# HGRN2 attention and rational MoE: units of one batch, decay products on GpSimd, a new order

## The chip, the cores and the metric

The kernel runs on one NeuronCore of a Trainium2 chip. Its five engines work at the same time, each through its own queue in order: TensorE (PE in the profile, with PEld for the weight loads), VectorE (DVE), ScalarE (ACT), GpSimd (POOL) and SyncE (SP). They wait for one another through semaphores. SP issues most of the loads and all stores; POOL issues the loads that change type, and the transfers that add. The metric is the device time of one execution in microseconds; lower is better.

## The reference

The input is 4 batches, 8 heads, 768 tokens, 48 values a head. First comes a linear attention with a decaying state, then a feed-forward layer (384 to 2048 to 384) whose activation is a quotient of polynomials:

```python
f = 1 / (1 + exp(-f_logit))
for t in range(S):
    state = f[:, :, t, :, None] * state + einsum('bhd,bhe->bhde', k[:, :, t], v[:, :, t])
    y[:, :, t] = einsum('bhd,bhde->bhe', q[:, :, t], state)
x = y.transpose(0, 2, 1, 3).reshape(B * S, H * D)
h = x @ w_in
P = a[0] + a[1]*h + a[2]*h**2 + a[3]*h**3
Q = 1 + abs(b[0])*abs(h) + abs(b[1])*h**2
out = (P / (Q + 1e-6)) @ w_out
```

## The kernel before

The work is cut into 12 units of 256 tokens. A unit `n` takes 128 successive tokens of two batches (j = 0 and 1). One partition holds two successive tokens of one batch, so that 64 partitions belong to each j. Units alternate between the two pairs of batches, and each pair has one state tile, renewed once a unit.

The order of the instructions is written out by hand: the string `ORDER` (lines 19 to 104) lists steps, and the loop at its end (line 560) issues them one by one. Each engine keeps this order in its own queue. `@0` to `@3` names one of four PSUM slots (two banks each). A step `name n ...` belongs to unit n.

The attention steps of a unit:

- `ld` loads f, k, q (SP) and v (POOL, as bf16), one transfer for each j (line 194). Unit 0 loads its heads in two halves.
- `ef` and `ls` (ACT, lines 279 and 284) make log(1 + exp(-f)) in place and into `lsp`; `cs` (PE, line 294) sums it over the tokens with triangular matrices; `A` (ACT, lines 304 and 306) takes exp of the sums, once for q (x = 0) and once for k (x = 1), each into one tile with a single buffer.
- `xa` (DVE, line 311) multiplies q or k by its `A`, 128x768 f32 by f32 into the bf16 tile `qkp`.
- `T` (PE, line 322) transposes them, `Te` (DVE, line 330) copies the result out of PSUM; `sc` (PE, line 343) forms the scores, `mk` (DVE, line 351) masks them; `vm` (POOL, line 358) packs a part of v.
- `ya` and `yb` (PE, lines 364 to 415) form y in PSUM from the state and from the scores, and the state's sum `sv`. `ae` and `st` (ACT and DVE, lines 425 and 429) multiply that by the last decay `alast` and give the next state. `ye` (ACT, line 420) copies y as the input xT of the feed-forward.

The feed-forward steps, over groups of 4 or 8 of the 16 column blocks:

- `h` (PE, line 438) multiplies by w_in; `hy` (ACT, line 452) copies to bf16; the square is formed by `sq` (DVE, line 456) or by `sa` (ACT, line 460); `ab` (DVE, line 464) takes the absolute value z.
- The denominator is the sum of square and z, and its logarithm is taken on ACT. The sum is formed in one of three ways: by `u`, identity matmuls into PSUM (line 472), read by `ln` (ACT, line 480); by `zv` on DVE (line 485); or by `zd`, a transfer that adds in SBUF (POOL, line 489). The last two are read by `lz` (ACT, line 496). `ex` (ACT, line 504) makes exp(-log).
- The numerator is formed on DVE by `p1`, `p2` and `pm` (lines 509, 514, 519), joined by `tv` (DVE, line 527) or by the adding transfer `ta` (POOL, line 523), and multiplied by `ex` in `gm` (DVE, line 532).
- `o` (PE, line 539) multiplies by w_out, `oe` (line 554) copies the result, `so` (SP, line 548) stores it.

Coefficients are scaled so that the denominator needs no multiplication: the scale of ScalarE's `ln` and the bias of its `A` for q are read from the tile `sig`. At the start VectorE clears whole padded tiles (`cz`), and POOL loads w_in in 8 transfers of 32 partitions (line 201) and w_out in 4 (line 205).

Of the kernel before, what the change touches and what calls it, by code (L numbers as in the profile page):

```python
# [19 lines left out]
cz 1; ld 0 v; ab_; ld 0 q 2 4; cz 0; ld 0 f 2 4; cz 2; cb; ld 0 f 0 2; wi 0 4; ld 0 k 2 4; fa  # L20
ld 0 k 0 2; cz 3; fb; ld 0 q 0 2; ef 0 2 4; ls 0 2 4; vm 0 0; ef 0 0 2; ld 1 f; vm 0 1; ls 0 0 2; ca
wi 4 16; cs 0 2 4 @0; cc; cs 0 0 2 @1; A 0 0 2 4; A 0 1 0 2; xa 0 0 2 4; A 0 1 2 4; A 0 0 0 2
xa 0 1 2 4; ld 1 k; xa 0 1 0 2; T 0 2 4 @1; xa 0 0 0 2; ld 1 q; Te 0 2 4; ld 1 v; T 0 0 2 @0
sc 0 1 @1; Te 0 0 2; ef 1; ld 2 f; mk 0 1; sc 0 0 @0; ya 0 @2 @3; ls 1; mk 0 0; yb 0 2 4; ae 0
cs 1 @1; st 0; yb 0 0 2; A 1 1; A 1 0; ye 0; h 0 0 4 @2; hy 0 0 4; h 0 4 8 @1; wo 4 8; wo 12 16
h 0 12 16 @2; hy 0 4 8; xa 1 1; ld 2 k; wo 0 4; h 0 8 12 @3; sq 0 0 8; wo 8 12; hy 0 12 16; ld 2 q
ab 0 0 8; hy 0 8 12; xa 1 0; u 0 0 4 @2; ab 0 8 16; T 1 @3; vm 1 0; ln 0 0 4; p1 0 0 8; ld 2 v
u 0 4 8 @1; Te 1; ef 2; ld 3 f; p2 0 0 8; sc 1 1 @3; vm 1 1; ln 0 4 8; sc 1 0 @2; mk 1 1; ls 2
ya 1 @1 @0; mk 1 0; ex 0 0 8; cs 2 @3; sq 0 8 16; yb 1; A 2 1; pm 0 0 8; u 0 12 16 @2; ye 1
p1 0 8 16; ae 1; A 2 0; h 1 0 4 @1; tv 0 0 8; ln 0 12 16; ld 3 k; h 1 12 16 @3; hy 1 0 4; p2 0 8 16  # L30
gm 0 0 8; h 1 4 8 @2; hy 1 12 16; pm 0 8 16; u 0 8 12 @1; hy 1 4 8; xa 2 1; h 1 8 12 @3; ln 0 8 12
tv 0 8 16; o 0 0 0 4 @2; ex 0 8 16; ab 1 0 8; o 0 1 0 4; sq 1 0 8; o 0 0 4 8; ld 3 q; hy 1 8 12
o 0 1 4 8; xa 2 0; u 1 0 4 @1; gm 0 8 16; T 2 @3; ld 3 v; ln 1 0 4; st 1; o 0 1 8 12; o 0 1 12 16
Te 2; ef 3; ld 4 f; vm 2 0; u 1 4 8 @0; vm 2 1; ls 3; sq 1 8 16; sc 2 0 @3; ln 1 4 8; sc 2 1 @1
ld 4 k; o 0 0 8 12; mk 2 0; o 0 0 12 16; ex 1 0 8; cs 3 @0; mk 2 1; ld 4 q; ab 1 8 16; A 3 1
ya 2 @1 @3; p1 1 0 16; A 3 0; vm 3 0; oe 0 0 2 s; yb 2; ld 4 v; xa 3 1; u 1 12 16 @0; ae 2; ye 2
so 0 0 2; p2 1 0 16; u 1 8 12 @2; ef 4; ld 5 f; vm 3 1; ln 1 12 16; h 2 12 16 @1; pm 1 0 8; ls 4
ld 5 k; st 2; h 2 0 4 @0; hy 2 12 16; tv 1 0 8; ln 1 8 12; cs 4 @3; ld 5 q; xa 3 0; h 2 4 8 @1
hy 2 0 4; gm 1 0 8; sa 2 0 4; h 2 8 12 @2; ld 5 v; pm 1 8 16; hy 2 4 8; o 1 0 0 4 @0; hy 2 8 12
ab 2 0 8; o 1 1 0 4; vm 4 1; tv 1 8 16; A 4 0; o 1 0 4 8; vm 4 0; ld 6 f; sa 2 4 8; T 3 @2  # L40
p1 2 0 16; A 4 1; o 1 1 4 8; ld 6 k; ex 1 8 16; xa 4 0; u 2 4 8 @1; Te 3; u 2 0 4 @3; ld 6 q
ln 2 4 8; gm 1 8 16; sc 3 1 @2; ln 2 0 4; sc 3 0 @1; mk 3 1; o 1 0 8 12; ef 5; o 1 1 8 12; mk 3 0
ex 2 0 8; o 1 1 12 16; ya 3 @2 @3; xa 4 1; ld 7 f; pm 2 0 8; ef 6; yb 3; ae 3; ls 5; T 4 @1; ld 7 k
st 3; vm 5 0; vm 5 1; ye 3; o 1 0 12 16; sq 2 8 16; ld 6 v; h 3 0 4 @2; oe 1 0 2 s; ld 7 q; Te 4
h 3 4 8 @0; so 1 0 2; hy 3 0 4; ab 2 8 16; ld 8 f; pm 2 8 16; ef 7; u 2 8 12 @1; hy 3 4 8; sc 4 0 @2
p2 2 0 16; h 3 8 12 @3; ln 2 8 12; ab 3 0 8; ta 2 8 16; u 2 12 16 @0; mk 4 0; hy 3 8 12; ta 2 0 8
cs 5 @1; ln 2 12 16; sq 3 0 8; sc 4 1 @2; h 3 12 16 @3; A 5 1; mk 4 1; zd 3 0 8; A 5 0; hy 3 12 16
xa 5 1; ya 4 @1 @0; ex 2 8 16; xa 5 0; ld 8 k; yb 4; p1 3 0 16; T 5 @3; ld 8 q; ld 7 v; ye 4
ab 3 8 16; ef 8; h 4 0 4 @1; Te 5; ae 4; ls 6; vm 6 0; h 4 4 8 @2; gm 2 8 16; vm 6 1; hy 4 0 4
ld 9 f; sa 4 0 4; pm 3 0 8; h 4 8 12 @3; hy 4 4 8; st 4; h 4 12 16 @1; hy 4 8 12; gm 2 0 8; sa 4 4 8  # L50
sc 5 1 @0; cs 6 @3; sq 3 8 16; hy 4 12 16; o 2 0 0 4 @2; ab 4 0 8; o 2 1 0 4; A 6 1; p2 3 0 16
zd 4 0 8; o 2 1 4 8; A 6 0; u 3 12 16 @1; lz 3 0 8; xa 6 0; ta 3 0 8; o 2 1 8 12; mk 5 1
o 2 1 12 16; ln 3 12 16; u 3 8 12 @3; xa 6 1; ld 9 q; ex 3 0 8; sc 5 0 @0; pm 3 8 16; o 2 0 4 8
ld 9 k; o 2 0 8 12; ab 4 8 16; ta 3 8 16; o 2 0 12 16; ln 3 8 12; p1 4 0 16; T 6 @1; oe 2 0 2 s
mk 5 0; ex 3 8 16; ya 5 @2 @3; so 2 0 2; pm 4 0 8; yb 5; ls 7; Te 6; ld 8 v; ae 5; cs 7 @0; ye 5
ld 10 f; st 5; sc 6 1 @1; lz 4 0 8; h 5 4 8 @2; mk 6 1; vm 7 0; vm 7 1; sc 6 0 @3; sq 4 8 16
hy 5 4 8; h 5 8 12 @1; A 7 0; gm 3 0 8; h 5 0 4 @2; A 7 1; zv 4 8 16; hy 5 8 12; o 3 0 0 4 @0
hy 5 0 4; o 3 0 4 8; pm 4 8 16; o 3 1 0 4; lz 4 8 16; mk 6 0; o 3 1 4 8; h 5 12 16 @2; p2 4 0 16
ef 9; ya 6 @3 @1; ex 4 0 8; ab 5 0 8; ta 4 0 8; gm 3 8 16; ta 4 8 16; yb 6; hy 5 12 16; sq 5 0 8
o 3 1 8 12; ye 6; o 3 1 12 16; p1 5 0 16; zd 5 0 8; ex 4 8 16; o 3 0 8 12; o 3 0 12 16; ld 9 v  # L60
sq 5 8 16; h 6 8 12 @3; ae 6; ls 8; st 6; h 6 12 16 @2; ef 10; vm 8 1; ld 11 f; pm 5 0 8; vm 8 0
hy 6 8 12; cs 8 @1; xa 7 1; hy 6 12 16; h 6 4 8 @3; ab 5 8 16; ld 10 k; oe 3 0 2 s; xa 7 0
u 5 12 16 @2; A 8 1; so 3 0 2; gm 4 0 8; A 8 0; T 7 @0; ld 10 q; ln 5 12 16; xa 8 0; u 5 8 12 @1
hy 6 4 8; Te 7; o 4 0 0 4 @2; ln 5 8 12; o 4 0 4 8; xa 8 1; sc 7 1 @0; sa 6 4 8; o 4 1 0 4
gm 4 8 16; sc 7 0 @1; lz 5 0 8; o 4 1 4 8; p2 5 0 16; o 4 0 8 12; o 4 0 12 16; mk 7 0; ex 5 8 16
ta 5 0 8; T 8 @3; mk 7 1; o 4 1 8 12; o 4 1 12 16; ex 5 0 8; sq 6 8 16; ya 7 @0 @1; pm 5 8 16
ld 11 k; oe 4 0 2 s; yb 7; ae 7; ls 9; Te 8; h 6 0 4 @2; ta 5 8 16; so 4 0 2; ye 7; vm 9 1; st 7
# [12 lines left out]
ls 11; so 6 0 2; cs 10 @3; vm 11 0; st 9; ye 9; u 8 4 8 @2; vm 11 1; gm 7 0 8; A 10 0; u 8 0 4 @0  # L80
A 10 1; pm 7 8 16; o 7 0 0 4 @1; ln 8 4 8; h 9 4 8 @3; sq 8 8 16; ta 7 8 16; ln 8 0 4; o 7 0 4 8
xa 10 0; sa 9 4 8; h 9 12 16 @0; p2 8 0 16; hy 9 4 8; o 7 1 0 4; ex 8 0 8; xa 10 1; ta 8 0 8
o 7 1 4 8; pm 8 8 16; h 9 0 4 @3; hy 9 12 16; gm 7 8 16; ta 8 8 16; T 10 @2; sa 9 0 4; zv 8 8 16
h 9 8 12 @0; hy 9 0 4; Te 10; lz 8 8 16; o 7 1 8 12; o 7 1 12 16; gm 8 0 8; sc 10 1 @2; sc 10 0 @3
hy 9 8 12; o 7 0 8 12; ab 9 0 8; o 7 0 12 16; mk 10 0; ex 8 8 16; zd 9 0 8; o 8 0 0 4 @0; p1 9 0 16
o 8 1 0 4; oe 7 0 2 s; o 8 1 4 8; ab 9 8 16; cs 11 @3; so 7 0 2; gm 8 8 16; ya 10 @1; A 11 0
o 8 0 4 8; mk 10 1; A 11 1; o 8 1 8 12; lz 9 0 8; o 8 0 8 12; xa 11 0; yb 10; sq 9 8 16; o 8 1 12 16
ye 10; o 8 0 12 16; xa 11 1; u 9 12 16 @2; ex 9 0 8; p2 9 0 16; T 11 @1; oe 8 0 2 s; h 10 4 8 @3
pm 9 0 8; ln 9 12 16; so 8 0 2; Te 11; h 10 12 16 @0; ta 9 0 8; hy 10 4 8; pm 9 8 16; sa 10 4 8
sc 11 1 @1; h 10 0 4 @2; mk 11 1; hy 10 12 16; ta 9 8 16; sc 11 0 @3; sa 10 0 4; ya 11 @0; mk 11 0  # L90
h 10 8 12 @1; hy 10 0 4; yb 11; ab 10 0 8; hy 10 8 12; u 9 8 12 @2; gm 9 0 8; ye 11; u 10 0 4 @1
# [21 lines left out]
def kernel(  # L113
# [22 lines left out]
    UB = 2  # L136
# [48 lines left out]
    def load(n, what, a0=0, a1=HP):  # L185
# [4 lines left out]
        if what not in s:  # L190
            s[what] = ld.tile([P, H, 2, D], dt, name=what + "n")
# [402 lines left out]
```

## Time and profile before

| | us |
|---|---|
| median of 3 runs (lowest, highest) | 247.41 (247.39, 249.63) |
| span of the profiled execution, first to last instruction | 244.1 |
| median less span | 3.3 |
| busy: PE, DVE, ACT, POOL | 214.6, 210.6, 204.8, 62.1 |
| `xa` of whole units on DVE, 22 | 21.0 |
| mean rate of the DMA engines | 155 GB/s |

The profile shows one execution. Of it the page gives the span; the time around the span is known only as the 3.3 us between it and the median of the runs. An engine is busy while one of its instructions runs; idle time of an engine is given with what released it. A row of the groups has the engine, the operation, the tiles and shapes, a count behind an x, then the busy time and the mean of one in ns, then the idle time ahead of it. A row of the waits has who waited for whom, the total, how often, and the longest. Transfers that add are listed under the POOL instruction that issues them.

### The profile page before, as it was taken

What the parts mean: (1) busy time and instruction counts of PE and PEld (TensorE: products, weight loads), DVE (VectorE), ACT (ScalarE), POOL (GpSimd) and SP (SyncE); (2) the same over time, 40 slices, a digit from 0 to 9 for tenths busy, and PEclk for the clock granted to TensorE, in tenths of its full rate; (3) what the DMA queues carried; (4) which work ended last, traced back from release to release, by engine and by line L of the source; (5) the groups of instructions that cost most, each with busy time, mean ns of one, the idle gap of its engine ahead of it and who ended that gap; (6) DMA issues with size and microseconds to landing.
All of it is one profiled execution on the core that took longest, in us unless ns stands there. A gap on an engine that the chain in (4) does not pass through costs nothing.

```text
span 244.1 us, 7193 instructions
## 1 busy us (share of the span) xinstructions
PE 214.6 (88%) x3144; PEld 146.9 (60%) x3144; DVE 210.6 (86%) x233; ACT 204.8 (84%) x213; POOL 62.1 (25%) x98
## 2 busy tenths in 40 slices
PE   0228787999998999997999999999999999999991
PEld 0115564765774868665668577668568658666550
DVE  7427179999999999999979999999999998899740
ACT  2422568989999899999799999999999999999930
POOL 7953201500400344233071032242122102004110
PEclk9999997999999999999999999999999999999997
DMA  6999999980799999999989999678529746606972
GB/s 82 217 199 198 204 196 221 208 131 0 127 208 204 166 239 169 201 200 220 161 161 165 232 179 172 101 153 131 105 74 172 145 97 118 121 3 129 199 145 64
DMA packets 61342, 37.94 MB, mean 155 GB/s; under 512 B 52096, under 2 KB 57600, under 8 KB 61312
## 3 DMA queue, kind: packets, MB, share of 16 engines
q0 software_dynamic: 19424, 18.62, 49.3%
q1 hardware_dynamic: 41888, 18.88, 40.1%
q8 instruction: 24, 0.39, 0.7%
q14 instruction: 6, 0.05, 0.1%
HBM read 25.17 MB, written 4.72 MB: 122 GB/s over the span
## 4 chain that ended last, share of the span: by engine, by line
PE 42%; ACT 18%; DMA 13%; DVE 13%; SPq 7%; issue 5%; DVEq 0%; ACTq 0%
PE op L539 15%; PE hp L438 13%; DMA fn<-in_f_logit_dram 8%; SPq L194 7%; DMA gall<-hy 5%; PE u L472 5%; ACT hy L452 4%; DVE gall L532 3%; ACT qi L504 3%; ACT lq L480 3%; PE y L364 2%; PE tp L322 2%; DVE h L456 2%; DVE gall L509 2%; PE sc L343 2%
## 5 line engine op out<-in xcount | busy, mean ns | idle before, releaser
L438 PE MATMUL hp<-xT,w_in_sb 128*128 128x256 bf16 x576 | 67.9, 273 | 1.7 <-ACT xT L420 1.4
L539 PE MATMUL op<-w_out_sb,gall 128*128 128x384 bf16 x384 | 68.4, 326 | 0.9 <-DVE osb L554 0.7
L438 PEld LDWEIGHTS <-w_in_sb 128*128 128x128 bf16 x576 | 55.4, 98 | 11.5 <-issue 2.1
L452 ACT CAST hy<-hp 128x1024 bf16<-128x1024 f32 x48 | 48.5, 1021 | 5.7 <-PE hp L438 5.4
L539 PEld LDWEIGHTS <-gall 128*128 128x128 bf16 x384 | 36.3, 98 | 25.5 <-DVE gall L532 1.2
L504 ACT ACTIVATE qi<-lq 128x2048 bf16<-128x2048 f32 (+1 forms) x25 | 46.5, 1871 | 0.2
L523 POOL DMA_DIRECT2D gall<-hy x21 | 19.5, 960 | 83.6 <-ACT hy L452 14.8
L480 ACT ACTIVATE lq<-u,sig 128x1024 f32<-128x1024 f32 x32 | 35.4, 1134 | 1.2 <-PE u L472 1.1
L532 DVE TENSOR_TENSOR gall<-gall,qi 128x2048 bf16<-128x2048 bf16 (+1 forms) x25 | 29.5, 1182 | 4.1 <-DMA gall<-hy 4.0
L351 DVE TENSOR_TENSOR scm<-sc,mask 128x1024 bf16<-128x1024 f32 x24 | 28.7, 1217 | 1.6 <-PE sc L343 1.6
L519 DVE TENSOR_TENSOR gall<-gall,h 128x2048 bf16<-128x2048 bf16 (+1 forms) x25 | 29.3, 1181 | 0.0
L194 POOL DMA_DIRECT2D vn<-in_v_dram x24 | 18.8, 801 | 27.0 <-issue 20.3
L456 DVE TENSOR_TENSOR h<-hy 128x2048 bf16<-128x2048 bf16 (+1 forms) x19 | 22.2, 1167 | 2.1 <-ACT hy L452 2.1
L294 PE MATMUL cs<-lsp,Ui 128*128 128x384 bf16 (+1 forms) x39 | 11.6, 359 | 12.5 <-ACT lsp L284 12.5
L358 POOL COPY vmp<-vn 128x128 bf16<-128x128 bf16 x24 | 10.7, 483 | 44.0 <-PE y L364 27.9
L279 ACT ACTIVATE fn<-fn 128x768 f32<-128x768 f32 (+1 forms) x13 | 10.7, 823 | 13.3 <-DMA fn<-in_f_logit_dram 13.3
L472 PE MATMUL u<-h,ident 128*128 128x512 bf16 x64 | 19.5, 387 | 0.0
L472 PEld LDWEIGHTS <-ident 128*128 128x128 bf16 x128 | 12.2, 99 | 11.7 <-issue 0.7
L472 PE MATMUL u<-z,ident 128*128 128x512 bf16 x64 | 19.1, 379 | 0.0
L322 PE MATMUL tp<-ident,qkp 128*128 128x128 bf16 x192 | 13.7, 227 | 6.0 <-DVE qkp L311 4.6
L509 DVE TENSOR_SCALAR gall<-hy,a_sb 128x4096 bf16<-128x4096 bf16 (+2 forms) x15 | 17.0, 1142 | 1.6 <-ACT hy L452 1.6
L311 DVE TENSOR_TENSOR qkp<-qn,A 128x768 bf16<-128x768 f32 (+1 forms) x13 | 11.6, 892 | 7.4 <-DMA qn<-in_q_dram 4.1
(70 smaller groups left out, 283.3 us busy)
## 6 DMA issues: line engine op xcount, KB each, us to landing
gall<-hy POOLq DMA_DIRECT2D x19, 512.0 KB, 6.1
fn<-in_f_logit_dram SPq DMA_DIRECT2D x22, 192.0 KB, 7.2
kn<-in_k_dram SPq DMA_DIRECT2D x22, 192.0 KB, 6.9
qn<-in_q_dram SPq DMA_DIRECT2D x22, 192.0 KB, 6.8
out_dram<-osb SPq DMA_DIRECT2D x22, 192.0 KB, 3.7
z<-h POOLq DMA_DIRECT2D x5, 512.0 KB, 6.2
vn<-in_v_dram POOLq DMA_DIRECT2D x24, 96.0 KB, 8.0
w_out_sb<-in_moe_w_out_dram POOLq DMA_DIRECT2D x4, 384.0 KB, 15.9
```

The lines of the kernel that those rows point to most:

```text
L194: eng.dma_start(out=s[what][R * j:R * j + R, hh].rearrange("p h i d -> p h (i d)"), in_=src[s["u"] * UB + j, hh, t0:t0 + C, :].rearrange(" ...
L351: nc.vector.tensor_mul(t, s["sc", g].rearrange("s r a i t -> s (r a) (i t)"), mb)
L438: nc.tensor.matmul(t[:, m - m0, :].rearrange("f (j t) -> f j t", j=UB), w_in_sb[:, kk, m * P:(m + 1) * P], s["x"][:, :, kk, :], start=(kk ...
L452: nc.scalar.copy(fl(big(s, "hy", "hy", 3), m0, m1), fl(s["hp", m0], 0, m1 - m0))
L456: nc.vector.tensor_mul(fl(big(s, "h2", "h2", 2), m0, m1), fl(s["hy"], m0, m1), fl(s["hy"], m0, m1))
L472: nc.tensor.matmul(t[:, m - m0:m - m0 + 2, :].rearrange("p m t -> p (m t)"), ident, fl(src, m, m + 2), start=(x == 0), stop=(x == 1))
L480: nc.scalar.activation(fl(s["lq", g], m0 - 8 * g, m1 - 8 * g), fl(s["u", m0], 0, m1 - m0), AF.Ln, scale=sig[:, 2:3], bias=1.0 + 1e-6)
L504: nc.scalar.activation(fl(s["qi", g], m0 - 8 * g, m1 - 8 * g), fl(s["lq", g], m0 - 8 * g, m1 - 8 * g), AF.Exp, scale=-1.0)
L509: nc.vector.tensor_scalar(fl(big(s, "g", "gall", 3), m0, m1), fl(s["hy"], m0, m1), a_sb[:, 3:4], a_sb[:, 2:3], op0=ALU.mult, op1=ALU.add)
L519: nc.vector.tensor_mul(fl(s["g"], m0, m1), fl(s["g"], m0, m1), fl(s["h2"], m0, m1))
L532: nc.vector.tensor_mul(fl(s["g"], m0, m1), fl(s["g"], m0, m1), fl(s["qi", g], m0 - 8 * g, m1 - 8 * g))
L539: nc.tensor.matmul(s["op"][:, j, 0:DM], s["g"][:, m, C * j:C * j + C], w_out_sb[:, m, :], start=(m == 0), stop=(m == KF - 1))
```

## The change

A unit is now 256 successive tokens of one batch, so j is the first or the second half of 256 tokens of the same batch. One load takes all 128 partitions. The state goes from j = 0 to j = 1 within the unit, so there are two state tiles for each batch, `st` has half the width and is done twice a unit, and `ya` is taken apart into `yi` (y from the state) and `sv`. From unit 1 on, `xa` runs on POOL. A step may carry a name at its end (`!m3`); an `xa` on POOL names one (`p m3`) and is made to begin behind it. Only unit 0 keeps `xa` on DVE, in four halves.

The scales that came from `sig` tiles are now registers of ScalarE, and the bias of `A` is gone (its factor is in `ye`). The memsets clear only the padding. w_in comes in 3 transfers of 128 partitions for each of two column ranges. The order is new: `sa`, `zv`, `tv` and half-size steps are no longer used; the unit's feed-forward uses `u` 24 times (32 before), `ln` 24 (32), `lz` 12 (8), `zd` 12 (5) and `ta` 24 (21, two of them half).

```diff
--- before
+++ after
-cz 1; ld 0 v; ab_; ld 0 q 2 4; cz 0; ld 0 f 2 4; cz 2; cb; ld 0 f 0 2; wi 0 4; ld 0 k 2 4; fa
-ld 0 k 0 2; cz 3; fb; ld 0 q 0 2; ef 0 2 4; ls 0 2 4; vm 0 0; ef 0 0 2; ld 1 f; vm 0 1; ls 0 0 2; ca
+cz 3; ab_ b a; ld 0 f 0 2; ld 0 v; ld 0 f 2 4; cz 1; cu 1; ld 0 k 2 4; cz 2; ci; ld 0 k 0 2; cu 0
+ld 0 q 2 4; ef 0 0 2; wi 4 16; cm; ld 0 q 0 2; ef 0 2 4; cz 0; fa; ls 0 2 4; ls 0 0 2; cs 0 2 4 @3; ld 1 v
...
+xa 1 1 0 4 p m1; A 1 0; yb 0 2 4; ld 2 k; yi 0 1; sv 0 1; ye 0 s; st 0 1; ef 2; h 0 12 16 @2; wi 0 4; ls 2
+ld 3 f; h 0 8 12 @1; hy 0 12 16; xa 1 0 0 4 p m1; cs 2 @3; hy 0 8 12; ld 2 q; A 2 1; wo 4 8; T 1 @2
+ab 0 8 16 !m3; A 2 0; xa 2 1 0 4 p m3; sv 1 0 @1; Te 1; h 0 4 8 @3; ab_ a s; ae 1; st 1 0; vm 1 0; sc 1 1 @2
...
+o 11 0 0 4 @3; o 11 1 0 4; oe 9 0 2 s; gm 11 8 16; o 11 1 4 8; oe 10 0 2 s; so 9 0 2 s; o 11 0 4 8
+o 11 1 8 12; so 10 0 2 s; o 11 0 12 16; o 11 0 8 12; o 11 1 12 16; oe 11 0 2 s; so 11 0 2 s
...
-            c, u = divmod(n, NU)
-            units[n] = dict(c=c, u=u, qk=qkp[n % 2], ls=lsp[n % 2], vm=vmp[n % 2], st=states[u])
+            c, b = divmod(n, B)
+            units[n] = dict(c=c, b=b, qk=qkp[n % 2], ls=lsp[n % 2], vm=vmp[n % 2], st=states[b])
...
-        for j in range(UB):
-            eng.dma_start(out=s[what][R * j:R * j + R, hh].rearrange("p h i d -> p h (i d)"),
-                          in_=src[s["u"] * UB + j, hh, t0:t0 + C, :].rearrange("h (p i) d -> p h (i d)", i=2))
+        eng.dma_start(out=s[what][:, hh].rearrange("p h i d -> p h (i d)"),
+                      in_=src[s["b"], hh, t0:t0 + NT, :].rearrange("h (p i) d -> p h (i d)", i=2))
...
-        if x == 0:
-            nc.scalar.activation(t, src, AF.Exp, scale=-1.0, bias=sig[:, 3:4])
-        else:
-            nc.scalar.activation(t, src, AF.Exp, scale=1.0)
+        nc.scalar.activation(t, src, AF.Exp, scale=1.0 if x else -1.0)
-    def xa(n, x, a0=0, a1=HP):
+    def xa(n, x, a0=0, a1=HP, eng="v", mark=None):
...
-        nc.vector.tensor_mul(s["qk"][:, x, :, hh, 0:D],
+        i = (nc.gpsimd if eng == "p" else nc.vector).tensor_mul(
+            s["qk"][:, x, :, hh, 0:D],
...
+        if mark is not None:
+            behind(i, mark)
+        return i
...
+    def coef_r():
+        for i in (0, 2):
+            regs[i] = nc.scalar.alloc_register(f"sig{i}")
+            nc.scalar.reg_load(regs[i], sig[0:1, i:i + 1].bitcast(U32))
...
+    def yi(n, j, sl=None):
+        s = unit(n)
+        y_open(s, sl)
+        for kk in range(KD):
+            for a in range(HP):
+                ymm(s, j, a, kk, s["st"][j][:, a, 32 * kk:32 * kk + 32], s["T"][:, 0, :, a, R * j:R * j + R])
...
-    def st(n):
-        s = unit(n)
-        nc.vector.tensor_mul(s["st"], s["sv"], _at(s["ae"], [[1, UB], [UB, HP], [0, 2 * D]]))
+    def st(n, j):
+        s = unit(n)
+        return nc.vector.tensor_mul(s["st"][1 - j], s["sv"][:, j], _at(s["ae"], [[UB, HP], [0, W]], j))
...
-                             scale=sig[:, 2:3], bias=1.0 + 1e-6)
+                             scale=regs[2], bias=1.0 + 1e-6)
...
+    def behind(i, mark):
+        tc.add_manual_dep(i.ins, marks[mark].ins.name,
+                          mybir.DependencyInfo(mybir.DependencyClass.Sync, mybir.DependencyReason.DATA),
+                          reason="begins behind it")
```

## The prediction

> **What bounds the kernel now.** I read the busy shares of the page first, then the table by stage, then the waits and the groups.
>
> ```profile
> PE 214.6 (88%) x3144; PEld 146.9 (60%) x3144; DVE 210.6 (86%) x233; ACT 204.8 (84%) x213; POOL 62.1 (25%) x98
> ```
>
> Three engines lie within 5% of each other, so the shares name no bound. I cut the span at the end of unit 1's copy `ye` (43 us) and at the next-to-last output copy (233.5 us).
>
> ```profile
> 0.00:43.00 43.00, 22.60 (x382) 15.37 (x383) 25.58 (x50) 19.88 (x27) 17.36 (x39) 0.97 1.18 188
> 43.00:233.50 190.50, 186.64 (x2733) 128.65 (x2732) 183.11 (x181) 183.63 (x185) 44.77 (x60) 1.00 0.86 151
> 233.50:244.10 10.60, 5.40 (x32) 2.87 (x30) 1.94 (x3) 1.29 (x3) 0.00 (x0) 0.87 0.43 97
> ```
>
> The columns are length, then busy time of PE, PEld, DVE, ACT and POOL, the granted clock, the DMA share and GB/s. In the middle PE is busy 98%, DVE and ACT 96% each: nothing is gained there unless all three get less to do. In the first 43 us they are busy about half, while the DMA moves 188 GB/s: the start waits for data. The waits say for which.
>
> ```profile
> ACT fn L279 <- DMA fn<-in_f_logit_dram: 13.3, 4, 7.9
> PE cs L294 <- ACT lsp L284: 12.5, 4, 10.0
> DVE qkp L311 <- DMA qn<-in_q_dram: 4.1, 2, 3.7
> DVE qkp L311 <- DMA kn<-in_k_dram: 3.9, 1, 3.9
> ```
>
> So there are two accounts: the start (order of loads) and the middle (work of three engines). The sum is made against the span of 244.1; the median of the runs, 247.41, is 3.3 more, and I carry that 3.3 over.
>
> **The middle, engine by engine.** Rows first (the last number ahead of the bar is the count; behind it busy us and mean ns):
>
> ```profile
> L311 DVE TENSOR_TENSOR qkp<-kn,A 128x768 bf16<-128x768 f32 x11 | 10.5, 958 | 3.9 <-DMA kn<-in_k_dram 3.9
> L311 DVE TENSOR_TENSOR qkp<-qn,A 128x768 bf16<-128x768 f32 x11 | 10.5, 952 | 0.6 <-DMA qn<-in_q_dram 0.4 <-ACT A L304 0.2
> L456 DVE TENSOR_TENSOR h<-hy 128x2048 bf16<-128x2048 bf16 x17 | 20.8, 1223 | 2.1 <-ACT hy L452 2.1
> L460 ACT ACTIVATE h<-hp 128x1024 bf16<-128x1024 f32 x12 | 12.6, 1053 | 0.2 <-PE hp L438 0.2
> L480 ACT ACTIVATE lq<-u,sig 128x1024 f32<-128x1024 f32 x32 | 35.4, 1134 | 1.2 <-PE u L472 1.1
> L496 ACT ACTIVATE lq<-z,sig 128x2048 f32<-128x2048 bf16 x8 | 16.2, 2024 | 0.0
> ```
>
> *PE.* The order forms the denominator by identity matmuls (`u`) 24 times, not 32. The chain shows one `u` as 0.86 us: 8 x 0.86 = 6.9 less. The sums for `alast` are made for 12 units, not 10: 16 matmuls more, 0.28 us for 8 in the chain. PE: -6.3.
>
> *ACT.* The 12 squares `sa` go (-12.6). `ln` falls from 32 to 24 (-9.1), `lz` rises from 8 to 12 (+8.1). The 11 whole `A` of q lose their bias, 921 against 828 ns (-1.0). An output copy comes back from DVE and `alast` has two more (+0.7). The scale of `ln`, now a register, I cost at nothing: both ends, 0 and 24 x 0.11 (the gap from the 1134 to the 1021 of `hy`) = -2.6, lie on an engine with slack. ACT: -14.
>
> *DVE.* 22 products `xa` leave (-21.0), so do 3 `zv` (-3.6), 4 `tv` (-4.9) and one output copy (-0.6). Squares rise from 20.8 + 1.4 to 24 x 1.223 (+7.2). The state product becomes 20 of half width; at 0.56 (a 128x384 copy from PSUM, 558 ns) that is 11.2 against 9.5 (+1.7). Fewer, longer `p1` and `p2` give -1.4; smaller memsets help only the start. DVE: -22.6.
>
> *What the 22 products cost on POOL.* No row shows POOL multiplying two f32 tensors. Ends: 0.95 us (the same work on DVE) and 3.5 us (POOL's copy `vmp`, 128x128 in 0.29 us, scaled by 768/128 and doubled for the second input). I take that copy scaled by size alone, 1.74 us, as the nearest row of that engine. 22 x 1.74 = 38 us on POOL, which is idle for 146 of the middle's 190 us; its 12 fewer loads of v at 0.80 take 9.6 back. So POOL has the time; the question is DVE:
>
> ```profile
> 42.34 0.81 DVE L509 TENSOR_SCALAR gall<-hy,a_sb 128x2048 bf16<-128x2048 bf16 x1
> 42.58 1.85 POOL L358 COPY vmp<-vn 128x128 bf16<-128x128 bf16 x1 [4.24 <-PE y L364]
> 43.06 1.22 DVE L527 TENSOR_TENSOR gall<-gall,hy 128x2048 bf16<-128x2048 bf16 x1
> 44.19 0.81 DVE L514 TENSOR_SCALAR hy<-hy,a_sb 128x2048 bf16<-128x2048 bf16 x1
> ```
>
> A POOL copy of 0.29 us took 1.85 us, and ended only as the two DVE steps over it did. DVE shut POOL out. Beside DVE steps that read PSUM (`mk` at 22.05 us, `st` at 23.87, 80.66 and 162.22) the same copy keeps 0.29 to 0.31 us. The other way round the trace shows little: the DVE steps over slow POOL copies grew by at most 0.2 us (a `p1` of 1.53 against 1.34), but those copies are short. I take it that a product beside a PSUM-reading step costs nothing, and beside any other holds DVE for all its length. The order places the 22 products ahead of: 18 times `mk`, `Te` or `st`, 4 times a step on SBUF. Adding the PSUM steps that follow each without a gap (`mk` and `Te` 1.22, `st` 0.56): five have 1.78, eight 1.22, five 0.56, four none, together 21.5 us of cover. Blocked: 38.3 - 21.5 = 17 us. Ends: 0 (POOL always yields or DVE is idle) and 77 - 21.5 = 56 (3.5 us each). DVE: -22.6 + 17 = -5.6.
>
> The Trainium skill ("SBUF — State Buffer", section "SBUF: two separate sides") says that DVE steps with two SBUF inputs or in a two-port mode and GpSimd steps hold one port pair exclusively, for the whole instruction. The row agrees (0.29 became 1.85). "GPSIMD Engine Reference", section 3, speaks against the change: it calls the engine the wrong choice for elementwise work, at 4497 ns for 2048 f32 pairs. An estimate from that page is 1.69 us for 768, which would make the blocked time 16 us and the sum 1 us less.
>
> *Waits that are added.* A product waits for its `A`, its load and its named step. In the order 13 of the 22 names lie over 30 DVE steps back; in the built program three products carry a wait on DVE. Behind a waiting product on POOL stand DMA additions `ta` and `zd`; `gm` (DVE) and `lz` (ACT) wait for those. `A` has one buffer, so ACT's next `A` waits for POOL as well. I price this at nothing, covered by the lead of the attention (units 2 and 3 are begun before unit 0's output): uncovered, it costs the 1.74 of a product for each, 38 us at most.
>
> *DMA.* Additions rise from 25 full-size equivalents to 36, +5.8 MB. The middle moved 151 GB/s x 190.5 = 28.8 MB; 34.6 MB in 184 us is 188 GB/s. Where additions and loads ran together (84 to 120 us) the four-microsecond windows of before show 170 to 263, so it fits, with little over. Half as many issues on SP (one per tensor) cost nothing.
>
> Sum of the middle: PE 186.6 - 6.3 = 180.3, ACT 169.6, DVE 183.1 - 5.6 = 177.5. The longest, PE, with its old 3.9 us of idle gives 184.2: **-6.3**. DVE with its old idle (7.4) would give 185, so the two bounds nearly meet.
>
> **The start.** SP's first load is now f of unit 0: its issue moves from 3.17 to 0.81 us, and ACT begins at 6.5, not 8.87. The six half loads of unit 0 are one issue each (0.65 us), out by 4.7, not 9.7; they and v are 1.4 MB, 7 us at 200 GB/s. The last q half then lands near 12.5, where DVE waited for it until 18.26. So unit 0's chain, and `h` (27.70 before), come 5.5 us earlier. After that three quarters of w_out stand behind the loads of units 2 and 3, for which ACT had waited at 37.6; of those waits I take 1.5 us off. Start: **-7**, ends 0 (the weights still collide) and -12 (the 13.3 of ACT's f waits nearly gone).
>
> **The tail.** The last output is copied whole on ACT (0.81) and not in halves by DVE and ACT (0.48 last): **+0.5**.
>
> 247.4 - 6.3 - 7 + 0.5 = **234.6, say 234.**
>
> **Rivals.** (1) *VectorE is blocked by the products* and becomes the bound; ends slower. DVE's middle is 160.5 + B, with its 7.4 of idle; start 36, tail 11.1 and 3.3 give 218 + B. PE's bound is 234, passed at B = 16; before is passed at B = 29, that is at 2.3 us a product with the cover, or at 1.74 if little is covered (B = 38: 256). For it: 19 products that no wait holds to their neighbours. Against: 18 good neighbours. About 253. (2) *POOL's queue is late*: additions stand behind products, `gm` and `lz` wait, and the middle keeps its 190.5; only the start is gained: 241. The DMA rate of 188 GB/s speaks for it. (3) *Order fills better than I count*: ACT and DVE get slack, so PE's 3.9 us of idle and more of the start go: 227. (4) *The products don't leave the path*, only change engine: that is the upper end of (1).
>
> **How the numbers follow.** Forecast 234 (230 to 238): 0.38. Rival 3 (below 230): 0.15. Rival 2 (238 to 245): 0.17, of which 0.01 falls within 1%. Rival 1, with (4): 0.23 slower by over 1%. Left: 0.07 within 1%, where (1) is at its weakest. One per cent, 2.5 us, is about what a measurement of this kernel can tell from no change. Faster 0.38 + 0.15 + 0.16 = 0.69, same 0.08, slower 0.23. The range leaves a tenth at each end: 222 (rival 3 with the start at -12) to 254 (rival 1).
>
> **What would show it.** Right: POOL's product rows near 1.74 us, DVE busy (blocked time shows as longer steps) near 200 of the span, ACT near 191; ACT's waits for f below 6 us; `h` of unit 0 near 22 us; PE still 97% in the middle. Wrong: `sq`, `pm`, `gm` means well above 1.22, by more than 29 us in all; waits of DVE on the DMA additions of more than 10 us; PE waiting in `T` for POOL's products.

## The result and the profile after

The changed kernel takes 260.03 us (median of 4 runs, 256.02 to 261.88) against 247.97 beside it: a ratio of **1.042, 95% interval 1.035 to 1.049**. It was forecast at 234 and is 4.2% slower than before. The profiled execution took 258.99, of which 257.3 are span: 13.2 more than the 244.1 of before. (The ratio stands for some 10 us; the traces lie further apart, since the profiled execution of before took less than the median, 245.8 by an estimate from its span.) Every ratio is against runs of the kernel before on the same chip and leaves disturbed executions out (in the run without additions, below, all but two of ten), so it can differ from the quotient of two medians. A point, below, is a hundredth of such a ratio.

The busy shares of the changed kernel, and then its table by stage (length, busy time of PE, PEld, DVE, ACT and POOL, granted clock, DMA share, GB/s), cut as before at 43 us and at the next-to-last output copy:

```profile
PE 220.1 (86%) x3128; PEld 151.5 (59%) x3128; DVE 202.0 (79%) x210; ACT 191.7 (75%) x197; POOL 110.9 (43%) x116
```

```profile
0.00:43.00 43.00, 22.73 (x390) 16.33 (x391) 19.21 (x47) 18.59 (x28) 20.30 (x31) 0.96 1.16 187
43.00:246.80 203.80, 192.94 (x2714) 132.72 (x2714) 181.57 (x163) 170.85 (x169) 90.63 (x85) 0.98 0.90 169
246.80:257.30 10.50, 4.42 (x28) 2.44 (x25) 1.23 (x1) 2.24 (x4) 0.00 (x0) 0.82 0.43 112
```

ACT and DVE lost what was forecast (191.7 and 202.0 busy). But PE, which was to fall by 6.3, rose by 5.5. By 43 us it has done 22.73 us of work, 22.60 before: the start gained nothing. After that there are 5.3 us more of work and 7.8 us more of idle time. The 13.2 us are therefore **5.5 us of PE work and 7.7 us of PE idle time**, all of it after the start.

*PE's work.* The groups of TensorE before, then after (count, busy us, mean ns, then the idle time ahead of them):

```profile
L539 PE MATMUL op<-w_out_sb,gall 128*128 128x384 bf16 x384 | 68.4, 326 | 0.9 <-DVE osb L554 0.7 <-DVE gall L532 0.2
L438 PE MATMUL hp<-xT,w_in_sb 128*128 128x256 bf16 x576 | 67.9, 273 | 1.7 <-ACT xT L420 1.4
...
L364 PE MATMUL y<-scm,vn 64*32 64x128 bf16 x384 | 10.5, 236 | 0.0
...
L395 PE MATMUL sv<-vn,qkp 64*64 64x48 bf16 x320 | 4.6, 192 | 0.0
```

```profile
L541 PE MATMUL op<-w_out_sb,gall 128*128 128x384 bf16 x384 | 71.4, 331 | 2.1 <-DVE gall L533 1.1 <-ACT hy L448 1.0
L434 PE MATMUL hp<-xT,w_in_sb 128*128 128x256 bf16 x576 | 70.5, 275 | 3.9 <-DMA w_in_sb<-in_moe_w_in_dram 2.0 <-issue 0.6 <-DVE scm L344 0.6
L357 PE MATMUL y<-scm,vn 64*32 64x128 bf16 x384 | 14.5, 226 | 0.2 <-ACT hy L448 0.2
...
L405 PE MATMUL sv<-vn,qkp 64*64 64x48 bf16 x320 | 9.2, 194 | 0.5 <-DMA vn<-in_v_dram 0.5
```

The same 384 small matmuls, no longer each, fill 14.5 us where they filled 10.5, and the 320 of `sv` fill 9.2 where they filled 4.6. In the rows, 64\*32 and 64\*64 are the parts of TensorE's 128\*128 array that one matmul uses. 384 matmuls of 236 ns that fill only 10.5 us overlap one another; my reading is that matmuls on different parts run at once when they are neighbours in the queue, which the first experiment tests. The change takes neighbours away: `yb` now covers two of the four pairs of heads at a time, and `sv` one half of the unit. The time in which any matmul of `y` ran went from 15.68 to 20.04 us, that of `sv` from 12.06 to 17.03, and that of `u` fell from 32.07 to 24.02. The two large groups, whose instructions are the same, took 5.6 us more, part of it at a lower clock (below). The sum 4.4 + 5.0 - 8.1 + 5.6, and 0.5 for the rest, is 7.4 and not 5.5, since groups overlap at their ends: the split is approximate.

*PE's idle time.* The waits of the changed kernel (who waited for whom, total, how often, longest), and SP's own queue:

```profile
POOL qkp L298 <- ACT A L293: 28.9, 4, 16.5
ACT fn L269 <- DMA fn<-in_f_logit_dram: 21.8, 4, 12.8
...
PE sc L336 <- ACT hy L448: 4.9, 1, 4.9
```

```profile
SPq L556 <- ACT osb L548: 152.4, 8, 34.8
```

The waits for f, 13.3 us before, are 21.8. Two places carry them. The first is the start, in the chain of work up to 45 us (start, length, what):

```profile
4.58 17.64 DMA fn<-in_f_logit_dram
...
22.25 0.85 ACT fn L269
...
28.27 1.24 PE hp L434 x11
29.51 9.17 DMA w_in_sb<-in_moe_w_in_dram
```

ACT began at 4.56 us (the forecast was 6.5) and `T` of unit 0 at 9.54 (13.99 before). But the order puts `ef 1` and `ls 1` ahead of `ae 0` on ACT, and f of unit 1 lands only at 22.2. So `alast`, the state, `y` and the first `h` of unit 0 (28.20 against 27.70 before) wait for a tensor that unit 0 doesn't need. Then w_in is missing: POOL issued its second part at 28.14, behind the first product, which waited 16.5 us for its `A`.

The second place is the middle. In the timeline of SP's queue (start, length, what) a store stands where nothing can pass it:

```profile
47.90 1.51 SPq L192 DMA_DIRECT2D qn<-in_q_dram  x1
84.18 1.36 SPq L556 DMA_DIRECT2D out_dram<-osb  x2
```

SP waited 34.8 us for unit 0's output, with loads of units 5 to 8 behind that store. The chain then shows f of unit 7 issued at 91.67 and used at 105.88; PE's 4.9 us in `sc` are for a `hy` that stands behind it on ACT:

```profile
91.67 14.19 DMA fn<-in_f_logit_dram
105.86 0.02 issue
105.88 0.84 ACT fn L269
```

What this stall does to PE, in stretches of 5 us (columns as in the table by stage):

```profile
100.00:105.00 5.00, 2.75 (x24) 2.17 (x23) 2.82 (x3) 0.00 (x0) 2.15 (x2) 1.00 1.28 204
105.00:110.00 5.00, 1.32 (x19) 0.84 (x19) 1.92 (x2) 4.12 (x5) 2.52 (x4) 0.67 1.10 229
110.00:115.00 5.00, 5.00 (x52) 2.44 (x54) 2.33 (x3) 2.54 (x3) 0.29 (x1) 0.65 1.15 278
115.00:120.00 5.00, 5.00 (x109) 3.00 (x109) 4.27 (x6) 4.57 (x5) 0.87 (x1) 1.00 1.13 231
```

PE is idle for 5.9 of 10 us, and then runs at a granted clock of 0.65: it is "busy" all 5 us to 115, with 52 matmuls against 109 in the next 5. An estimate from these rows: 6.3 busy us at 0.65 to 0.67 hold 4.2 us of work at full clock, so some 2 of PE's 5.5 us more are the clock.

*The products.* Groups of the changed kernel:

```profile
L452 DVE TENSOR_TENSOR h<-hy 128x2048 bf16<-128x2048 bf16 x24 | 33.9, 1417 | 1.0 <-ACT hy L448 0.9
L533 DVE TENSOR_TENSOR gall<-gall,qi 128x2048 bf16<-128x2048 bf16 x24 | 31.8, 1333 | 3.6 <-DMA gall<-hy 1.9 <-ACT qi L501 1.7
...
L298 POOL TENSOR_TENSOR qkp<-qn,A 128x768 bf16<-128x768 f32 x11 | 23.9, 2177 | 9.1 <-ACT A L293 3.4 <-DMA qn<-in_q_dram 3.1 <-ACT lsp L274 2.5
...
L298 POOL TENSOR_TENSOR qkp<-kn,A 128x768 bf16<-128x768 f32 x11 | 21.7, 1969 | 35.3 <-ACT A L293 25.5 <-DMA kn<-in_k_dram 5.9 <-issue 3.8
```

The shortest product took 1.80 us, and 45.6 us went to all 22. DVE's steps grew beside them: `sq` 1223 to 1417 ns, `gm` 1224 to 1333, `pm` 1223 to 1272, `ab` 688 to 843, `p2` 1338 to 1528. Times their counts that is 4.7 + 2.6 + 1.2 + 3.7 + 2.3 = 14.5 us.

### The profile page after: what moved, and what is told of

Same layout as the page of the kernel before. It is cut to its first block, busy times and chain, and to the rows that moved or that the text cites. A ratio compares the mean times of both kernels' runs of the same rounds, so it can differ in the third digit from the quotient of the medians.

```text
span 257.3 us, 7089 instructions
## 1 busy us (share of the span) xinstructions
PE 220.1 (86%) x3128; PEld 151.5 (59%) x3128; DVE 202.0 (79%) x210; ACT 191.7 (75%) x197; POOL 110.9 (43%) x116
## 4 chain that ended last, share of the span: by engine, by line
PE 51%; DMA 16%; DVE 16%; ACT 9%; SPq 3%; issue 2%; POOL 0%; ACTq 0%; DVEq 0%
PE op L541 17%; PE hp L434 15%; DMA fn<-in_f_logit_dram 12%; PE y L357 6%; PE u L468 5%; DVE h L452 4%; DMA w_in_sb<-in_moe_w_in_dram 4%; ACT hy L448 3%; SPq L192 3%; PE tp L314 2%; DVE gall L533 2%; DVE z L460 2%; DVE qkT L322 2%; PE cs L284 2%; PE sc L336 2%
## 5 line engine op out<-in xcount | busy, mean ns | idle before, releaser
L501 ACT ACTIVATE qi<-lq 128x2048 bf16<-128x2048 f32 x24 | 45.9, 1921 | 0.1
L298 POOL TENSOR_TENSOR qkp<-kn,A 128x768 bf16<-128x768 f32 x11 | 21.7, 1969 | 35.3 <-ACT A L293 25.5
L452 DVE TENSOR_TENSOR h<-hy 128x2048 bf16<-128x2048 bf16 x24 | 33.9, 1417 | 1.0 <-ACT hy L448 0.9
L533 DVE TENSOR_TENSOR gall<-gall,qi 128x2048 bf16<-128x2048 bf16 x24 | 31.8, 1333 | 3.6 <-DMA gall<-hy 1.9
L520 DVE TENSOR_TENSOR gall<-gall,h 128x2048 bf16<-128x2048 bf16 x24 | 30.4, 1272 | 0.0
L460 DVE TENSOR_SCALAR z<-hy 128x2048 uint16<-128x2048 uint16 x24 | 20.0, 843 | 12.2 <-ACT hy L448 10.9
L298 POOL TENSOR_TENSOR qkp<-qn,A 128x768 bf16<-128x768 f32 x11 | 23.9, 2177 | 9.1 <-ACT A L293 3.4
L269 ACT ACTIVATE fn<-fn 128x768 f32<-128x768 f32 (+1 forms) x13 | 10.5, 804 | 21.8 <-DMA fn<-in_f_logit_dram 21.8
L479 ACT ACTIVATE lq<-u 128x1024 f32<-128x1024 f32 x24 | 24.0, 1031 | 2.3 <-PE u L468 1.9
L293 ACT ACTIVATE A<-cs 128x768 f32<-128x768 f32 (+1 forms) x26 | 18.6, 761 | 6.9 <-PE cs L284 6.7
L493 ACT ACTIVATE lq<-z 128x2048 f32<-128x2048 bf16 x12 | 23.0, 1914 | 0.0
```

The lines of the kernel that those rows point to most:

```text
L298: i = (nc.gpsimd if eng == "p" else nc.vector).tensor_mul(s["qk"][:, x, :, hh, 0:D], s["qk"[x]][:, hh].rearrange("p h i d -> p i h d"), s[ ...
L452: return nc.vector.tensor_mul(fl(big(s, "h2", "h2", 2), m0, m1), fl(s["hy"], m0, m1), fl(s["hy"], m0, m1))
L460: return nc.vector.tensor_scalar(fl(big(s, "z", "z", 2), m0, m1).bitcast(U16), fl(s["hy"], m0, m1).bitcast(U16), 0x7FFF, None, op0=ALU.bit ...
L479: nc.scalar.activation(fl(lq(s, g), m0 - 8 * g, m1 - 8 * g), fl(s["u", m0], 0, m1 - m0), AF.Ln, scale=regs[2], bias=1.0 + 1e-6)
L493: nc.scalar.activation(fl(lq(s, g), m0 - 8 * g, m1 - 8 * g), fl(s["z"], m0, m1), AF.Ln, scale=regs[2], bias=1.0 + 1e-6)
L501: nc.scalar.activation(fl(s["qi", g], m0 - 8 * g, m1 - 8 * g), fl(s["lq", g], m0 - 8 * g, m1 - 8 * g), AF.Exp, scale=-1.0)
```

## The experiments

Theory P: lost neighbours on TensorE cost the time. Theory Q: late data does, by two queue faults; the expectations call them S (loads behind a store) and F (the start). Theory R: POOL's products do, by blocking DVE. Theory M, later: several of these hide one another. All but M are put to the changed kernel first, one edit each.

**P alone.** `y` whole from unit 1 on, as before:

```diff
         y_open(s, sl)
+        if n > 0:
+            if a0 == 0:
+                return
+            a0 = 0
```

> The changed kernel, but from unit 1 on the second half step of y does both halves, so that its 64 matmuls stand together over four column groups and two row groups, as before the change. Theory P (small matmuls lost their neighbours; y costs 20.0 us of PE here, 15.7 before): PE's time in y falls to 16 to 17 us, and the kernel is 2 to 5 us faster than the changed one, since PE is busy 97% from 120 us on. Theory S (loads stand behind a store in SP's queue) and theory R (VectorE blocked by the products): y falls too, but the time stays within 1.5 us of the changed kernel, about 259.

Measured: 257.36 us, ratio 1.041 (1.033 to 1.049). `y` fell to 15.64 us of PE as it had been, and the ratio didn't move (1.042). The packing is the cause of the longer `y`, shown; but none of the 4.4 us is seen in the time (the interval would hide some 2). PE as a whole was busy 217.3 us, 2.8 less.

**Q, the stores.** Every store one output later in SP's queue:

```diff
-oe 0 0 2 s; ... so 0 0 2 s; ... oe 1 0 2 s; ... so 1 0 2 s
+oe 0 0 2 s; ... oe 1 0 2 s; so 0 0 2 s; ... oe 2 0 2 s; so 1 0 2 s
```

> The changed kernel, but each store is issued one output copy later in the order, so that loads no longer stand behind a store that waits for its copy (34.8 us for the first). Theory S: the 12.8 and 6.4 us waits of ACT and the gap of 100 to 108 us go for the second of them; the kernel is 5 to 9 us faster than the changed one, 250 to 254. Theory P and theory R: loads come earlier, but the time changes by less than 2 us.

Measured: 256.17, ratio 1.038 (1.030 to 1.047). SP's longest wait for an output fell from 34.8 to 24.0 us, the second stall for f is gone (ACT's waits for f: 15.9, of which 13.1 are the start), and the time is at most a little better.

**Q, the start.** Unit 0's `ae` and `ye` ahead of unit 1's `ef` and `ls`, and w_in's second part ahead of the first product:

```diff
-mk 0 1; ld 2 f; ef 1; Te 0 0 2; ls 1; sv 0 0 @0; ... ae 0; cs 1 @2; ... ye 0 s; ... h 0 12 16 @2; wi 0 4
+mk 0 1; ld 2 f; Te 0 0 2; sv 0 0 @0; ... ae 0; ... ye 0 s; st 0 1; wi 0 4; ef 1; ls 1; h 0 12 16 @3; cs 1 @2
```

> The changed kernel, but in the start the exp and log of unit 1's f stand behind unit 0's copy of y on ACT, and the second part of w_in is issued by POOL ahead of the first product. Theory F (unit 0 waits behind unit 1's f in ACT's queue, and w_in behind a product in POOL's): unit 0's first h begins near 20 us and not at 28.2, and the kernel is 3 to 7 us faster than the changed one. If the transfers bound the start (200 GB/s whatever the order): h begins earlier, but the time changes by less than 2 us.

Measured: 258.05, ratio 1.042 (1.033 to 1.051). The first `h` came at 21.3 us, where the forecast had it, and then waited for w_in. By 43 us PE had done 23.78 us of work, 1.05 more. It isn't seen in the time.

**R.** All products back on VectorE, in the changed order:

```diff
-xa 1 1 0 4 p m1
+xa 1 1 0 4
```

> The changed kernel, but all products of q and k stay on VectorE. Theory R (the products on GpSimd, by blocking VectorE and by holding POOL's queue, are the loss): 8 to 13 us faster than the changed kernel, back to 247 to 251. Theories P, S and F: VectorE takes 21 us more and loses 14 us of longer steps, with 55 us of idle time to take it; the time changes by less than 4 us, 256 to 263.

Measured: 255.78, ratio 1.035 (1.028 to 1.042), with DVE busy 206.8 and POOL 65.1. Theory R's 247 to 251 is out. The products on POOL gain nothing here; whether they lose is within the spread. DVE's steps, in the same order without products beside them, are short again:

```profile
L439 DVE TENSOR_TENSOR h<-hy 128x2048 bf16<-128x2048 bf16 x24 | 29.3, 1225 | 1.1 <-ACT hy L435 1.0
```

`sq` takes 1225 ns, `gm` 1216, `pm` 1214, `ab` 696 and `p2` 1408. By this comparison the products lengthened them by 13.7 us (14.5 above, against the old order).

No single fault is the loss. So the parts were tried the other way round, put into the kernel before. **The packing alone:** `y` in halves, `sv` half by half.

```diff
-yb 1
+yb 1 0 2; yb 1 2 4
-for a in range(HP): for i in range(2): for j in range(UB): ...   (sv)
+for j in range(UB): for a in range(HP): for i in range(2): ...
```

> The kernel before, but with the changed kernel's grouping of small matmuls alone: y of units 1 to 11 in two halves of two column groups each, and the sums sv and the y from the state one half of the tokens after the other. Theory P (small matmuls that lose their neighbours cost PE 9.4 us, and PE bounds the middle): PE's time in y and sv rises by 6 to 10 us, and the kernel takes 5 to 10 us more, 252 to 257. If the lost neighbours are hidden by waits: under 2 us more.

Measured: 247.69, ratio **1.009 (1.004 to 1.015)**. Of its groups:

```profile
L348 PE MATMUL y<-scm,vn 64*32 64x128 bf16 x384 | 11.9, 225 | 0.3 <-DVE scm L335 0.3
L348 PE MATMUL y<-scm,vmp 64*32 64x128 bf16 x384 | 10.2, 224 | 0.0
...
L379 PE MATMUL sv<-vn,qkp 64*64 64x48 bf16 x320 | 6.2, 192 | 0.0
```

10.5, 8.6 and 4.6 before became 11.9, 10.2 and 6.2; with all of `y` and `sv`, 3.0 us more (15.68 to 17.10, 12.06 to 13.64), and some 2.3 us (0.93% of 245.7; the interval is 0.9 to 3.6) came through to the time. Where PE is 98% busy, its work counts. But it is less than theory P had, 6 to 10 us: here the two halves of `y` follow each other at once, while in the changed order other matmuls stand between them (at 65.8 us, `u`), and that arrangement wasn't tried here.

**The products alone:** POOL takes them in the order before, with no thought for neighbours.

```diff
-        nc.vector.tensor_mul(s["qk"][:, x, :, hh, 0:D],
+        (nc.gpsimd if n > 0 else nc.vector).tensor_mul(s["qk"][:, x, :, hh, 0:D],
```

> The kernel before with its own order, units and names, but from unit 1 on the products of q and k are formed by GpSimd. Theory R (the products on GpSimd are the loss): VectorE's other steps are lengthened by 20 to 30 us and additions come late; 8 to 15 us more than before, 255 to 262. Theory P: VectorE loses 21 us of work and gains 15 to 25 us of longer steps, PE stays the bound; within 4 us of before, 243 to 251.

Measured: 258.64, ratio **1.054 (1.049 to 1.059)**. Its busy shares, then its groups:

```profile
PE 214.9 (83%) x3129; PEld 146.7 (57%) x3144; DVE 221.5 (86%) x211; ACT 204.9 (79%) x213; POOL 111.3 (43%) x120
```

```profile
L519 DVE TENSOR_TENSOR gall<-gall,h 128x2048 bf16<-128x2048 bf16 x23 | 35.2, 1533 | 0.0
...
L456 DVE TENSOR_TENSOR h<-hy 128x2048 bf16<-128x2048 bf16 x17 | 24.9, 1463 | 7.3 <-ACT hy L452 7.3
L311 POOL TENSOR_TENSOR qkp<-kn,A 128x768 bf16<-128x768 f32 x11 | 24.8, 2253 | 30.5 <-DMA kn<-in_k_dram 15.5 <-ACT A L306 15.1
```

DVE gave away 21.0 us and is 10.9 us *busier*: its steps are 31.9 us longer in all (221.5 less 210.6 - 21.0), 1.45 us for each of 22 products. In the changed order it is 14.5 us, 0.66 each. That fits the prediction's reading that a product beside a step that reads PSUM costs little: in the timelines such steps stand over some 21 of the products' 46 us in the changed kernel, and over some 6 of 48 us here. It is argued, not shown: the two orders differ in more than that, and no run has the changed order without its named steps. (The prediction counted only three products whose name became a wait on DVE, so what matters would be the order and not the names.)

**All mends together,** the first three edits in one kernel, and then the same **with the products on VectorE**:

```diff
-y in halves; so n right behind oe n; ef 1, ls 1 ahead of ae 0; wi 0 4 behind the first xa
+y whole; so n behind oe n+1; ae 0, ye 0 ahead of ef 1, ls 1; wi 0 4 ahead of the first xa
-xa n x 0 4 p m..        (second kernel only)
+xa n x 0 4
```

> The changed kernel with all three edits at once: y whole, stores one output copy later, unit 0 ahead of unit 1's f and w_in ahead of the products. One at a time they gave nothing that stands clear of the spread. If the losses lie in one another's shadow (theory M), together they give more than their sum: 246 to 252, PE's time down by 4 and its idle time by 5 or more. If something else holds the kernel (theory R, or the order as such), 254 to 259.

> As the run with all three edits, and the products on VectorE too. Theory R: 5 us or more below the run with all three edits. Theory M: within 3 us of it, either way, since VectorE's 21 us of products stand against 14 us of longer steps.

Measured: 253.53, ratio 1.032 (1.027 to 1.037), and 250.9, ratio 1.023 (1.018 to 1.028). The mends bring 1.0 point together, and the time lies between what the two theories had. Products on VectorE bring 0.9 more in the mended order: POOL costs some 2 us there and gains nothing. By 43 us PE had done 24.95 and 26.09 us of work (22.60 before): the earlier start is real, 2.3 to 3.5 us of busy time (the second at a granted clock of 0.92, so a part of its 3.5 is slower work), and is lost again behind it. 2.3% stay. `hp` and `op` still take 72.0 and 71.1 us here, 6.7 more than before; why isn't shown.

**What is left: PE's work in `sv`?** The last kernel, with the products of both halves of `sv` issued together:

```diff
-for a ...: for i ...: for par ...:                (half j)
+for a ...: for i ...: for jj in range(UB): for par ...:    (both halves, in step sv n 0)
```

> On the kernel with all three mends and the products on VectorE (250.9 us, sv 17 us of PE), the products of keys and values for both halves of the unit are issued together (four neighbours on TensorE instead of two), and the second half only adds its state later. Theory that PE work is what is left of the loss: sv falls by 3 to 5 us, PE busy from 216.9 to about 213, time to 247 to 249. Rival, that PE has idle gaps which take up the saving: sv falls as much, the time stays within 1 us of 250.9.

Measured: `sv` fell from 17.00 to 13.68 us, though it issues 384 of these products and not 320; 253.99, ratio 1.018 (1.007 to 1.030), not to be told from 1.023. The rival, gaps that take up PE's saving, fits better than the theory's 247 to 249, but the interval is too wide to rule out a gain of a point.

**What is left: the additions by DMA?** The changed order has 36, the kernel before 26. They are left out in the mended kernel with products on VectorE, and in the kernel before (the outputs of these runs lack what the additions would add):

```diff
-ta 0 0 8; ... zd 0 8 16; ... (every ta and zd)
```

> The same kernel (all mends, products on VectorE) with the 36 additions made by DMA left out: the denominator's square and the numerator's second half are then missing from the output, and PE, ACT and VectorE do the same work as before. Theory that the additions, landing 6.5 us after their issue and 18.9 MB of transfers, hold up the middle: time falls from 250.9 to about 240 to 244, and loads land earlier. Rival, that they are covered: within 2 us of 250.9.

> The kernel before with its 26 additions made by DMA left out in the same way (the same parts of the output are missing, for the units that use them). Theory that the 36 additions of the changed order cost more than the 26 here: time falls by 1 to 3 us only, so that the gap to the changed order without additions nearly closes. Rival, that the additions cost both alike or nothing: this one falls as much as the changed order does, and the gap of about 5 us stays.

Measured: the kernel before falls to 243.49, ratio 0.987 (0.979 to 0.995). The changed order has a median of 248.46, but its ten executions spread from 243.41 to 251.01. Its two lowest (243.41, 245.05) have a mean of 244.23, 0.991 of 246.49, the mean of the kernel before beside them; its median is 1.010 of the 245.98 beside it. In stretches of 43 to 80 and 120 to 160 us, first the mended kernel with additions, then without, then the kernel before without:

```profile
43.00:80.00 37.00, 32.72 (x527) 23.99 (x529) 35.25 (x37) 31.14 (x33) 7.41 (x9) 1.00 1.13 216
...
120.00:160.00 40.00, 37.68 (x545) 26.68 (x546) 34.84 (x36) 32.02 (x34) 9.82 (x14) 0.96 1.02 197
```

```profile
43.00:80.00 37.00, 34.78 (x568) 25.55 (x566) 36.62 (x39) 32.98 (x35) 8.79 (x11) 1.00 0.80 144
...
120.00:160.00 40.00, 39.79 (x572) 28.10 (x571) 38.37 (x39) 35.87 (x38) 6.70 (x6) 1.00 0.47 93
```

```profile
43.00:80.00 37.00, 35.91 (x448) 23.98 (x446) 36.34 (x36) 34.96 (x38) 5.22 (x8) 0.98 0.96 150
...
120.00:160.00 40.00, 40.00 (x634) 27.56 (x631) 39.45 (x39) 39.93 (x39) 4.78 (x8) 1.00 0.43 81
```

Without additions PE gains 2.06 and 2.11 us there, and comes near the kernel before; by 200 us it is 3.2 us ahead, since in the first 43 us it did 1.5 less. By the two lowest executions the additions cost the changed order 3.2 points (1.023 to 0.991) and the kernel before 1.3, and without them the two kernels lie 0.7 us apart (244.23, 243.49). By the medians they cost 1.1 points (250.9 is 1.021 of 245.71) and 1.0, and the two stay 5.0 us apart (248.46, 243.49). So whether the additions are behind the 2.3% that are left hangs on two executions of ten. Two runs ask where they cost, by leaving out 12 of the 36:

```diff
-(every ta and zd of units 0 to 3)        second run: of units 8 to 11
```

> The kernel with all mends and the products on VectorE (250.9 us), with the 12 additions of units 0 to 3 left out (their squares and second halves are then missing from the output). In the profile of the kernel with all 36 left out, TensorE gained 4.2 us in the stretches 43 to 80 and 120 to 160 us. Theory that the additions cost where they collide with the early loads and the weights: these 12 give back most of what the 36 gave, 3 to 5 us, so 246 to 248. Rival, that every addition costs the same 0.19 us: 2.3 us, so 248.6. Second rival, that the additions cost nothing in fact: within 1 us of 250.9.

> The same kernel with the 12 additions of units 8 to 11 left out instead, where the engines move 27 to 150 GB/s. Theory of the collision: within 1 us of 250.9. Rival of an equal cost for each: 2.3 us less, so 248.6.

Measured on one chip: 248.57, ratio 1.002 (0.997 to 1.007), and 250.9, ratio 1.010 (1.004 to 1.017). The kernel with all 36 ran on another chip, where the kernel before had a median of 245.71 and not 247.76 as here, so its 1.023 can't be set beside these ratios without care. By the medians alone the early 12, beside the loads and weights, cost 2.3 us and the late 12 nothing (250.9 with all 36). The first is what equal costs had, the second what the collision had, and the intervals of the two ratios touch: neither theory holds cleanly. That the early additions cost something is likely; that the additions are more of a burden to the changed order than to the old one isn't shown, and the early additions of the kernel before weren't left out alone. What holds the last 2.3% stays open.

**One part of the change by itself:** registers for ScalarE's scales, no bias in `A`, in the kernel before.

```diff
-                             scale=sig[:, 2:3], bias=1.0 + 1e-6)
+                             scale=regs[2], bias=1.0 + 1e-6)
```

> The kernel before with one part of the change alone: the scales of the logarithms and of the copy of y are registers of ScalarE, and the bias of the factor for q is gone. ACT loses 0.1 us in each of 32 + 8 logarithms and 0.1 in each whole factor, some 5 us of 204.8. Theory that in the middle ScalarE is as much a bound as TensorE: time falls by 1 to 3 us. Rival, that TensorE alone sets the end: within 1 us of the kernel before.

Its logarithm, 1134 ns before:

```profile
L480 ACT ACTIVATE lq<-u 128x1024 f32<-128x1024 f32 x32 | 32.4, 1038 | 2.1 <-PE u L472 2.0
```

Measured: ratio 0.998 (0.993 to 1.002). ACT lost 4.1 us (204.8 to 200.7) and the time at most 0.7 points, 1.7 us. So ACT, 96% busy in the middle, isn't what sets the end by itself; the theory's 2 to 3 us are out, its 1 us is not. No kernel tried that computes everything beats the kernel before.

## Why the prediction was wrong

- **"PE: -6.3" failed**, and it was the step that the sum rested on. It measured +5.5. I counted matmuls that go (`u`, which gave 8.1 and not 6.9, since the 32 of before ran for 32.07 us, 1.00 each, and 0.86 was the length of one in the chain) and priced those that stay at their old time. The small ones stay, nearly the same in number, and lose their neighbours: +9.4 in their own time, with the means no longer. `hp` and `op`, which I took as unchanged, took 5.6 more, some of it at a lower clock and the rest unexplained. The diff shows both splits, and I passed over them.
- **"The longest, PE, with its old 3.9 us of idle" failed.** The idle time isn't a constant that a new order inherits: after the start it grew by 7.8 us. The run that took 4.4 us out of `y` and gained nothing says that PE no longer sets the middle's length alone.
- **"Half as many issues on SP cost nothing" failed.** The issues are cheap, but a store waits in the same queue: 34.8 us in one piece, 20.9 before. Mended alone it gave 0.3 points, within the spread; all mends together gave 1.0.
- **"Start: -7" failed by the queue, not by the loads.** ACT and `T` were even earlier than forecast, and with `ae 0` ahead of `ef 1` the first `h` came at 21.3, near the forecast 22. The step left out what stands ahead of unit 0's own work on ACT, and w_in behind a waiting product on POOL. It is mis-sized as well: mended, the start is worth 2.3 to 3.5 us of PE work by 43 us.
- **"I price this at nothing" (the added waits) failed in kind, mildly in size.** POOL waited 28.9 us for `A`, and w_in stood behind the longest of these waits. With the blocking the products cost some 2 us in the mended order.
- **"It fits, with little over" (DMA) isn't settled.** The rate fits (169 GB/s in the middle). The additions aren't free, 1.3 points in the kernel before, and 1.1 to 3.2 in the changed order by the two ways of reading its executions. Whether the ten more of them are part of the loss is open.
- **ACT -14 held** (191.7 for 190.8), **DVE -22.6 + 17 held** (202.0 for 205; blocked 14.5 for 17), and a product at **1.74** measured 1.80 at the least, 2.07 in the mean. The estimate of 1.69 from the Trainium skill ("GPSIMD Engine Reference", section 3) lies 6% below that floor; it would not have taken 1 us off the sum, as I wrote, since the sum went by PE. The section's rule to use VectorE for elementwise work holds here: in the mended order the products are 0.9 points better off there. The **tail** (+0.5) measured -0.1.
- **The 3.3 carried over** was not all time around the span. In every run on record the time exceeds the span of the same execution by 1.6 to 1.8 us; the rest is that the profiled execution of before was shorter than the median.
- **Rivals.** Of the first, slower by blocking, the mechanism is real (5.4% in the order before), but it isn't what made this kernel slow: DVE is 79% busy, and the products cost some 2 us. The second, POOL's queue late, named a part; it had the middle keep its 190.5 us, and the middle took 203.8. No rival had PE's own work grow, or loads shut in behind a store, so the range's upper end, 254, was passed.

## What to carry to other kernels

Price the instructions that stay as well: when a reorder or a split takes away a small matmul's neighbours, its group grows while its mean does not. For every queue that is executed in order, ask of the new order what stands *behind* each wait: a load behind a store or weights behind a waiting product are shut in, however early they were written. And before adding a saving on the busiest engine to the sum, see that this engine has no idle time in the new order that would take it up.

## What was not expected of the hardware

- The granted TensorE clock after a stall: 0.65 to 0.67 in the 10 us around the one at 105 us, with half the matmuls done in 5 "busy" us. A stall of 5.9 us so costs more than its length, and the busy time hides it: `hp` and `op`, the same 960 instructions, took 5.6 us more in the changed kernel, part of it here (an estimate of 2 us for all groups).
- POOL's products and DVE's steps on SBUF slow each other: a product of 1.80 us took up to 3.45, and one product cost DVE 1.45 us in the order before, where its neighbours weren't chosen, and 0.66 in the changed order.
- A ScalarE logarithm of 128x1024 takes 1134 ns with its scale from a tile and 1031 to 1038 with it from a register.
